# Decode attention backward on one Trainium2 core: two dV stores cut into a large part and two unequal rests

## The chip, the cores and the metric

The kernel runs on one core of a Trainium2 chip. The metric is the device time in microseconds (us) of one execution; lower is better. The core's engines run side by side: TensorE (PE, matrix products), VectorE (DVE), ScalarE (ACT), GpSimd (POOL) and SyncE (SP, which here only issues transfers), and 16 DMA engines that move data between the device memory (HBM) and the on-chip memory (SBUF, 128 partitions).

## The reference

One step of decode attention and its gradient: 32 heads, one query row each, 8192 keys and values of width 128, all bfloat16.

```python
def _fwd_reference(q, k, v):                  # q 1x32x1x128, k and v 1x32x8192x128
    scale = q.shape[-1] ** -0.5
    scores = jnp.einsum('bhqd,bhkd->bhqk', q, k) * scale
    attn = _softmax(scores, axis=-1)
    return jnp.einsum('bhqk,bhkd->bhqd', attn, v)

def reference(q, k, v, grad_out):
    ...
    _out, _vjp = jax.vjp(_f, q, k, v)
    _grads = _vjp(grad_out)
    return (out, dq, dk, dv)                  # in short
```

For a head with probabilities p (8192 of them) the outputs are out = p v, dV = p (outer) grad_out, dp = v grad_out, dS = p (dp - sum of p dp) times the scale, dQ = dS k and dK = dS (outer) q. K and V are read once (2 MB each for a head) and dK and dV of the same size are written, so every head moves 4 x 2 MB.

## The kernel before

**Layout.** A head's K lies in a tile `Kt` of 128 partitions x 64 slots x 128 numbers; partition p holds rows 64p to 64p + 63 of the head, which are 16 KB in one piece both in HBM and in the partition. `Vt` and the two gradient tiles `G_dk` and `G_dv` have the same layout. A load or store of a whole head is one transfer of 128 rows of 16 KB, issued by SyncE (`load_k`, L81; `load_v`, L85; the stores in `outer`, L266). K has three buffers, V two, each gradient two.

**Work of a head.** In the loop over h (0 to 32), step h does the first half of head h and the second half of head h - 1, in an order written out by hand (`tc.manual_schedule()`): VectorE transposes K in four blocks (`k_blocks`, `XK_sb`, L162), TensorE forms the scores (`k_scores`, L177), VectorE and ScalarE the softmax (`e`, `nbias`, `p_rep`), TensorE transposes V (`v_transposes`, L197) and forms dp (`v_scores`, L207), and `contract` (L231) accumulates out and dQ (`acc_p`, `acc_ds`). In between VectorE writes the outer products: `outer(h, which, r)` makes quarter r (16 slots) of dK or dV of head h in one VectorE instruction (L256) of 128 x 2048 numbers. After the last quarter it issues the store. For the first and the last head the store goes in two halves; for all others it is a single transfer after quarter 3:

```python
        if r % (4 // parts) == 4 // parts - 1:
            c = r // (4 // parts)
            nc.sync.dma_start(rows_of(dst, h, c, parts), slots(G, c, parts))
```

**Order on SyncE's queue.** In a step h: the store of dK of head h - 1 (after its quarter 3), the load of V of head h + 2 (`load_v`, in front of quarter 3 of dV), the store of dV of head h, then, in the next step, the load of K of head h + 3 (`load_k`), and so on. A load waits until its buffer is free, that is, until TensorE has done with the K or V that lay there. A first quarter of dV of head h writes a tile whose last store was that of head h - 2, and waits for that store. At the end `result` (L302) stores the two small outputs, 32 rows of 256 B each, from `fin_sb`; `out_0` in step 31 behind the stores of dV of head 31, `out_1` behind the stores of dK of head 31.

The functions that the change touches:

Of the kernel before, what the change touches and what calls it, by code (L numbers as in the profile page):

```python
# [19 lines left out]
K_BUFS = 3  # L20
V_BUFS = 2
QD = 32


@with_exitstack
def kernel(
# [11 lines left out]
    nc = tc.nc  # L38
    P = 128
    _, H, S, D = k.shape  # L40
    assert D == P and S % (P * CH) == 0 and H <= P
    NT = S // P
    NCH = NT // CH
    NQ = P // QD
    assert NCH == 4 and NQ == 4
    W = D // 2
    NB = W // QD
    scale = float(D) ** -0.5
# [20 lines left out]
    def rows_of(x, h, c, parts):  # L69
        L = NT // parts  # L70
        return x[0, h].rearrange("(p n) d -> p n d", p=P)[:, c * L:(c + 1) * L, :]

    def slots(X, c, parts):
        L = NT // parts
        return X[:, c * L:(c + 1) * L, :]
# [26 lines left out]
    nc.vector.memset(ones_f[:], 1.0)  # L102
    do_win = consts.tile([P, H, 2, QD + 2], BF16)
    nc.gpsimd.memset(do_win[:], 0.0)
    wins = {}
    for which in ("p", "ds"):
        wins[which] = []
        for i in range(2):
            w = consts.tile([P, NG, 2 * QD - 4], BF16, name=f"win_{which}{i}")
            nc.gpsimd.memset(w[:], 0.0)  # L110
            wins[which].append(w)
    q_win = []
    for i in range(2):
        w = consts.tile([P, 2 * NB, P + QD], BF16, name=f"win_q{i}")
        nc.gpsimd.memset(w[:], 0.0)
# [5 lines left out]
    q_blk = consts.tile([P, H, 2 * NB, NQ], BF16)  # L121
    four = consts.tile([H, 2 * NB, NQ, QD], BF16)
    for w in range(NB):
# [125 lines left out]
    def outer(h, which, r):  # L249
        x = st[h]  # L250
        if r == 0:
            x[which] = gpool.tile([P, NT, D], BF16, tag=which, name="G_" + which)
        G, dst = x[which], out_2 if which == "dk" else out_3
        rep, row = x["ds"] if which == "dk" else x["p"], qd[h][:, 0 if which == "dk" else 1, :]
        Q = NT // 4
        nc.vector.tensor_tensor(  # L256
            slots(G, r, 4).rearrange("p n (a b) -> p n a b", b=R),
            slots(rep, r, 4).unsqueeze(2).to_broadcast([P, Q, D // R, R]),
            row.rearrange("p (a b) -> p a b", b=R).unsqueeze(1).to_broadcast([P, Q, D // R, R]),
            op=ALU.mult)  # L260
        parts = 1
        if h == 0 or h == H - 1:
            parts = 2
# [3 lines that stand above are left out]
# [37 lines left out]
    for h in range(H + 1):  # L304
# [18 lines left out]
        if h > 0:  # L323
            ds_of(p_)
            outer(p_, "dk", 0)
            dq_of(p_, 0)
        if h < H:
            s_back(h)
        if h > 0:
            dq_of(p_, 1)  # L330
            outer(p_, "dk", 1)
            if p_ % ST == ST - 1:
                gather_copy("ds")
                gather(p_, "ds", st[p_]["m"])
# [9 lines left out]
        if h > 0:  # L344
            outer(p_, "dk", 2)
# [83 lines left out]
```

## Time and profile before

| What | us |
|---|---|
| median of 3 runs | 642.45 (642.36 to 643.0) |
| the profiled execution, whole | 642.33 |
| its span, first to last instruction | 640.5 |
| VectorE busy | 546.7 (85%) |
| TensorE busy | 466.5 (73%) |
| ScalarE busy | 205.5 (32%) |
| HBM read and written | 134.23 MB each, 419 GB/s over the span |

The profile's page gives busy times, the span in 40 slices, the DMA queues, the chain of waits that ended last, the costliest groups of instructions and the DMA issues. Other views answer questions on one stretch of time. In the slices each digit is the busy share of a slice in tenths; "DMA" is the mean busy share of the 16 DMA engines and "GB/s" what they moved. A view of one window divides that window into 40 slices. Times in views are from the span's start. The trace also records every packet of the DMA engines (start, length, size, queue, without the number of the engine) and every increment of a semaphore: each DMA engine that takes part in a transfer writes one such mark of 4 bytes when its share is done, and the transfer has landed when all its marks are there.

### The profile page before, as it was taken

To read this page: it belongs to the slowest core of one execution; us is meant where nothing else is said; L and a number is where in the kernel's file an instruction comes from. 1 tells how busy PE (TensorE), PEld (TensorE's weight loads), DVE (VectorE), ACT (ScalarE), POOL (GpSimd) and SP (SyncE) were. 2 spreads that over 40 slices of the span, in tenths; PEclk is the share of its full clock that TensorE was granted. 3 is DMA by queue.
4 is the path that set the end of the run, shared out by engine and by line. 5 is a ranking of instruction groups with operands and counts; after the bars stand their busy time and mean duration, and the time that the engine had idled before them with its cause. 6 is when DMAs were issued, how large, how long until landed. Compare 5 with 4: busy or idle time off the path is not lost.

```text
span 640.5 us, 8426 instructions
## 1 busy us (share of the span) xinstructions
PE 466.5 (73%) x3336; PEld 276.5 (43%) x3336; DVE 546.7 (85%) x780; ACT 205.5 (32%) x507; POOL 7.1 (1%) x13
## 2 busy tenths in 40 slices
PE   3776778778877867887866867767877687676771
PEld 1444444445544533455533444434554344444351
DVE  6799999998999999988889888898888988889871
ACT  1433332234433322334421333313442133322240
POOL 4000000000000000000000000000000000000000
PEclk9979888887787899877899887898787888879875
DMA  8999999999999999999999999999999999999994
GB/s 353 421 415 427 429 431 426 425 433 426 429 431 427 429 431 427 430 429 429 431 427 432 428 425 437 427 424 436 428 425 435 428 426 434 426 430 433 427 405 193
DMA packets 19671, 269.01 MB, mean 420 GB/s; under 512 B 2352, under 2 KB 2352, under 8 KB 2864
## 3 DMA queue, kind: packets, MB, share of 16 engines
q1 hardware_dynamic: 19536, 268.46, 98.6%
q8 instruction: 26, 0.43, 0.3%
q14 instruction: 13, 0.11, 0.0%
q10 hardware_dynamic: 96, 0.02, 0.0%
HBM read 134.23 MB, written 134.23 MB: 419 GB/s over the span
## 4 chain that ended last, share of the span: by engine, by line
DMA 45%; DVE 39%; PE 9%; ACT 4%; issue 1%; DVEq 0%; ACTq 0%
DMA Kt<-in_k_dram 45%; DVE XK_sb L162 15%; DVE G_dv L256 9%; DVE G_dk L256 7%; PE s_ps L177 3%; DVE dpT L214 2%; PE T_ps L197 2%; PE acc_ds L231 2%; ACT XV_sb L188 2%; DVE sT L184 1%; ACT p_rep L371 1%; DVE prod L217 1%; DVE ds L285 1%; ACT qd L273 1%; DVE four L125 1%
## 5 line engine op out<-in xcount | busy, mean ns | idle before, releaser
L197 PE MATMUL T_ps<-ident_f,Vt 128*128 128x128 f32 x1024 | 178.0, 339 | 1.0 <-DMA Vt<-in_v_dram 0.4
L256 DVE TENSOR_TENSOR G_dv<-p_rep,qd 128x2048 bf16<-128x2048 bf16 x128 | 148.2, 1220 | 35.3 <-DMA out_dram<-G_dv 28.1
L177 PE MATMUL s_ps<-XK_sb,win_q 128*128 128x512 bf16 x512 | 135.8, 397 | 50.1 <-DVE XK_sb L162 26.3
L197 PEld LDWEIGHTS T_ps<-ident_f,Vt 128*128 128x128 f32 x1024 | 151.4, 177 | 28.5 <-issue 20.1
L256 DVE TENSOR_TENSOR G_dk<-ds_rep,qd 128x2048 bf16<-128x2048 bf16 x128 | 154.7, 1210 | 1.1
L188 ACT COPY XV_sb<-T_ps 128x512 f32<-128x512 f32 x256 | 138.4, 586 | 53.2 <-PE T_ps L197 52.6
L162 DVE STREAM_TRANSPOSE XK_sb<-Kt 128x1024 f32<-128x1024 f32 x128 | 151.4, 1221 | 3.1 <-DMA Kt<-in_k_dram 2.9
L177 PEld LDWEIGHTS <-win_q 128*128 128x128 bf16 x512 | 52.7, 105 | 123.8 <-issue 83.2
L290 ACT COPY win_ds<-ds 128x64 bf16<-128x64 bf16 x32 | 7.8, 244 | 193.0 <-DVE ds L285 193.0
L355 ACT ACTIVATE e<-sT,nbias 128x64 f32<-128x64 f32 x32 | 13.0, 406 | 138.4 <-DVE nbias L350 138.4
L343 PE MATMUL m_ps<-ident_f,top 128*128 128x128 f32 x32 | 11.0, 342 | 60.3 <-DVE top L341 57.3
L207 PE MATMUL dp_ps<-XV_sb,do_win 128*32 128x512 bf16 x512 | 34.0, 382 | 24.7 <-ACT XV_sb L188 24.7
L231 PE MATMUL acc_p<-Vt,win_p 128*32 128x512 bf16 x512 | 48.3, 516 | 0.5 <-ACT win_p L372 0.5
L343 PEld LDWEIGHTS m_ps<-ident_f,top 128*128 128x128 f32 x32 | 4.5, 139 | 74.4 <-DVE top L341 72.9
L231 PE MATMUL acc_ds<-Kt,win_ds 128*32 128x512 bf16 x512 | 33.5, 382 | 0.9 <-ACT win_ds L290 0.9
L207 PEld LDWEIGHTS <-do_win 128*32 128x32 bf16 x512 | 14.2, 94 | 36.0 <-issue 29.5
L369 DVE RECIPROCAL rinv<-m_ps 128x1 f32<-128x1 f32 x32 | 5.4, 168 | 24.9 <-ACT qd L273 24.9
L184 DVE STREAM_TRANSPOSE sT<-s_ps 128x512 f32<-128x512 f32 x32 | 22.7, 709 | 3.6 <-PE s_ps L177 3.6
L356 PE MATMUL m_ps<-rs,ones_f 128*128 128x1 f32 x64 | 15.4, 310 | 11.5 <-ACT e L355 11.5
L231 PEld LDWEIGHTS <-win_p 128*32 128x32 bf16 x512 | 13.1, 117 | 23.8 <-issue 12.2
L214 DVE STREAM_TRANSPOSE dpT<-dp_ps 128x512 f32<-128x512 f32 x32 | 21.6, 675 | 0.8 <-PE dp_ps L207 0.8
L356 PEld LDWEIGHTS m_ps<-rs,ones_f 128*128 128x128 f32 x64 | 14.0, 272 | 17.8 <-ACT e L355 17.3
(57 smaller groups left out, 203.3 us busy)
## 6 DMA issues: line engine op xcount, KB each, us to landing
Vt<-in_v_dram SPq DMA_DIRECT2D x32, 2048.0 KB, 29.5
Kt<-in_k_dram SPq DMA_DIRECT2D x31, 2048.0 KB, 31.6
out_dram<-G_dv SPq DMA_DIRECT2D x30, 2048.0 KB, 34.8
out_dram<-G_dk SPq DMA_DIRECT2D x30, 2048.0 KB, 32.2
out_dram<-G_dv SPq DMA_DIRECT2D x4, 1024.0 KB, 11.6
out_dram<-G_dk SPq DMA_DIRECT2D x4, 1024.0 KB, 11.7
Kt<-in_k_dram SPq DMA_DIRECT2D x4, 512.0 KB, 5.6
out_dram<-fin_sb SPq DMA_DIRECT2D x2, 8.0 KB, 12.1
```

Of the source, the lines that this page charges most:

```text
L162: nc.vector.transpose(XK[h][:, :, :, u, :], slots(Kt[h], u, NCH).rearrange("p g d -> p (g d)").bitcast(F32).rearrange("p (g w j) -> p g w ...
L177: nc.tensor.matmul(st[h]["s"][:], lhsT=q_win[h % 2][:, c, at:at + P], rhs=cols[:, c // 2, u, c % 2], start=(u == 0 and c == 0), stop=(u == ...
L184: nc.vector.transpose(sT[:].rearrange("p g r -> p (g r)"), x["s"][:])
L188: nc.scalar.copy(XV[h][:, c * TB:(c + 1) * TB, :], st[h].pop(("T", c))[:])
L197: nc.tensor.transpose(T_ps[:, i, :], words[:, m * P:(m + 1) * P], ident_f[:])
L207: nc.tensor.matmul(out[b * QD:(b + 1) * QD, :], lhsT=do_win[:, h, e2, 2 - 2 * z:2 - 2 * z + QD], rhs=cols[:, z, e2, :, b * QD:(b + 1) * QD ...
L214: nc.vector.transpose(x["dpT"][:].rearrange("p m r -> p (m r)"), x["dp"][:])
L231: nc.tensor.matmul(acc[which][b * QD:(b + 1) * QD, :], lhsT=window(h, which)[:, g, at:at + QD], rhs=X[:, 4 * g:4 * g + 4, :].rearrange("p ...
L256: nc.vector.tensor_tensor(slots(G, r, 4).rearrange("p n (a b) -> p n a b", b=R), slots(rep, r, 4).unsqueeze(2).to_broadcast([P, Q, D // R, ...
L343: nc.tensor.transpose(x["m"][:, 128:256], top[:].to_broadcast([P, P]), ident_f[:])
L355: nc.scalar.activation(e[:].rearrange("p (u g) -> p u g", u=NCH), x["sn"], ACT.Exp, bias=nbias[:], scale=scale, accum_out=rs[:])
L356: nc.tensor.matmul(x["m"][:, 0:1], lhsT=ones_f[:], rhs=rs[:], start=True, stop=True, skip_group_check=True)
```

## The change

In `outer`, the dV stores of heads 20 and 24 leave in three transfers each instead of one. For head 20 the first has 48 of the 64 slots of all 128 partitions (rows of 12 KB); the other 16 slots (rows of 4 KB) go as partitions 0 to 123 and partitions 124 to 127. For head 24 the first has 56 slots (rows of 14 KB); the other 8 (rows of 2 KB) go as partitions 0 to 122 and 123 to 127. All three are issued after quarter 3, where the single store was. Everything else stays.

```diff
+SPLIT = {20: (16, 124), 24: (8, 123)}
...
             row.rearrange("p (a b) -> p a b", b=R).unsqueeze(1).to_broadcast([P, Q, D // R, R]),
             op=ALU.mult)
+        if which == "dv" and h in SPLIT:
+            if r == 3:
+                n, c = SPLIT[h]
+                to = dst[0, h].rearrange("(p n) d -> p n d", p=P)
+                nc.sync.dma_start(to[:, 0:NT - n, :], G[:, 0:NT - n, :])
+                for a, b in ((0, c), (c, P)):
+                    nc.sync.dma_start(to[a:b, NT - n:NT, :], G[a:b, NT - n:NT, :])
+            return
         parts = 1
         if h == 0 or h == H - 1:
             parts = 2
```

## The prediction

> **What bounds the kernel now.** The slices of the span come first.
>
> ```profile
> DVE  6799999998999999988889888898888988889871
> DMA  8999999999999999999999999999999999999994
> GB/s 353 421 415 427 429 431 426 425 433 426 429 431 427 429 431 427 430 429 429 431 427 432 428 425 437 427 424 436 428 425 435 428 426 434 426 430 433 427 405 193
> ...
> q1 hardware_dynamic: 19536, 268.46, 98.6%
> ```
>
> The 16 DMA engines are busy from the second slice to the last but one, at about 429 GB/s, and one queue (q1, SyncE's) carries it all. No engine that computes is near that. The chain of waits says the same in its last part: a K load of 32 us, a few us of work that lead to the next K load's issue, and so on.
>
> ```profile
> 567.39 31.98 DMA Kt<-in_k_dram
> 599.38 0.02 issue
> 599.40 3.50 DVE XK_sb L162 x3
> ```
>
> A load that takes 32 us where 2 MB need 4.9 us at 429 GB/s stands in a queue: about 27 us of older transfers are ahead of it. So a few us more or less in the issue of a transfer mean nothing; what counts is how much each of the 16 engines has to carry. They are not level. The DMA view of the last 16 us, in 40 slices of 0.4 us:
>
> ```profile
> DMA  6589998999999896422222111000000000000000
> GB/s 287 246 369 411 437 471 369 430 410 431 410 411 471 370 471 254 187 108 123 102 102 102 64 82 63 22 41 20 20 20 41 20 20 41 1 0 0 0 0 0
> ```
>
> One engine moves 429/16 = 26.8 GB/s. From 631.8 us some four engines are left (102 GB/s), after 635 us a single one (20 to 41), which works on to 638.9 us. SyncE waits for it:
>
> ```profile
> SPq L424 <- DMA out_dram<-fin_sb: 11.2, 1, 11.2
> ```
>
> The trace's landing records give every engine's place, since each engine writes one done-mark for each transfer (the page's 2,352 packets under 512 B are 139 x 16 marks and 128 rows of 256 B). The marks of the first small store, issued at 621.87, come after the first of them by 0, 0, 0, 0.1, 0.3, 2.0, then 3.9, 4.1, 4.2, 4.2, 4.3, 4.3, then 6.3, 7.1, 7.6, and 11.4 us. At the V load that lands at 23 us the same spread was an even ladder from 0 to 0.7 us. Two things made the lags. The page's code fetches (q8: 26 packets, q14: 13) each hold up the engine they fall on: a 16 KB fetch takes some 1.09 us and the packet behind it 1.08 instead of 0.61, so 1.6 us. And the last engine falls back steadily, from 5.0 us at 277 to 11.1 at 603: 1.9% slower than the rest in the long stretch (many of its 16 KB packets take 621 ns and more, for 611 elsewhere). Every load waits for its slowest engine, so this one also paces the chain.
>
> **The change, part by part.** It takes a quarter of head 20's dV store (0.5 MB) and an eighth of head 24's (0.25 MB) out of the two 2 MB stores, and sends them as stores of 124 + 4 and 123 + 5 rows. The bytes are the same, and the arithmetic is untouched.
>
> *What the remaining big stores save.* In every transfer of the trace the 16 engines take equal shares: 8 of 128 rows each. That stays so for the 48- and 56-slot parts. Packet times from the records: 611 ns for 16 KB, 309 for 8 KB, 159 for 4 KB, so 75.5 ns for each 2 KB between 8 and 16. Rows of 12 KB take 460 ns: 8 x 151 = 1.21 us less on each engine. Rows of 14 KB: 8 x 75.5 = 0.60 us less. Together 1.81 us for each engine that gets none of the small stores; 1.84 on the slow one.
>
> *Where the cut rows go.* No transfer of before has a row count that 16 doesn't divide. Bounds: dealt over all 16 engines (7 or 8 rows each), the change moves nearly nothing; all 124 rows on one engine would be 124 x 156 ns = 19.3 us. I take equal shares, since that is the only dealing the trace shows: 124 = 4 x 31 rows, 4 = 4 x 1, 123 = 3 x 41, 5 = 5 x 1. Packets follow each other 3 ns before the end of the last, so a 4 KB row costs 156 ns. Head 20 puts 31 x 156 + 156 = 4.99 us on four engines, with two marks 5.0, net of the saving +3.8. Head 24 puts 41 rows of 2 KB on three: about 81 ns each, on the line between 15 ns for 256 B and 159 for 4 KB (ends: 64 if only bytes counted at 159/4, 75.5 by the slope above, 156 if a row cost as much as 4 KB), so 3.3 + 0.1, net +2.8. Three engines get 6.6 us more (at 156 ns a row, 9.7), a fourth about +3.2, a fifth -0.5 for head 24, the rest -1.81.
>
> *Which engines.* The records carry no engine number. What they show: four of the five level engines at 598 us stand at 0, 0.06, 0.10, 0.15 us, which are the first rungs of the ladder at 23 us (0, 0.03, 0.07, 0.09, 0.12). So the engines served first in each transfer are those that no code fetch held up. If a transfer on few engines takes the first ones too, the load falls on engines with 11 us to spare. That is my choice.
>
> The Trainium skill, "DMA: Bandwidth & Descriptors", section "Why a DMA increments its semaphore by 16 and not by 1", says how the number of engines is chosen (the largest number up to 16 that divides both slowest dimensions) and that they are the lowest-numbered ones; no run here shows engine numbers. By it the dealing would be 4, 4, 3 and 5 engines. The same page speaks against such stores: "Rules for kernel authors" wants all 16 engines used through an outermost dimension that is a multiple of 16, and calls splitting a transfer by partitions pointless. If the extra 6.6 us stood on the path, that rule would make it 642.45 + 6.6 = 649.1, an estimate.
>
> *The sum.* Slow engine: 638.88 - 1.84 = 637.04. Loaded engines, if level: through with everything before the last two dK stores at 622.8 us, they now get there at 629.4, then carry 4.9 us (two 1 MB stores of 16 x 0.306 us in all), and end at 634.3, 2.7 us before the slow one. The next in line, 3.6 us ahead of the slow engine before, loses 1.81 as well. So the slow engine still ends last, 1.84 us earlier, and the loads at the end land as much earlier. Profiled execution: 642.33 (span 640.5 and 1.8 around it) - 1.84 = 640.5; the median of the runs shown is 0.12 higher, so 640.6.
>
> *Edits at nothing.* Two more issues on SyncE in each of two heads, 0.33 us each. Queued behind them is only the next K load, which waits for `acc_ds` anyway (issue of the store at 440.23, of the load at 448.00):
>
> ```profile
> SPq L81 <- PE acc_ds L231: 194.4, 28, 7.4
> ```
>
> Without that cover 4 x 0.33 = 1.3 us would come under 27 us of queue. The first product of dV of heads 22 and 26 now waits for three stores instead of one on VectorE, with the next head's K transposes queued behind it and TensorE's K scores behind those. It waits for the last mark, which is the slow engine's as long as the loaded ones lag less: 0.1 + 3.8 against 8.2 - 1.2 where head 20's store lands, 0.1 + 6.6 against 10.1 - 1.8 where head 24's does. So no wait gets longer.
>
> **The rivals.** *Slower: a loaded engine is one that already lags.* With +6.6 us an engine sets the end at its own lag + 6.6 against the 11.4 of before: below 3.0 us of lag nothing is lost, from 4.8 us on the kernel becomes slower. The three at 6.3, 7.1 and 7.6 would give +1.5 to +2.8 (644 to 645.3), the slow engine itself +6.6 (649). Drawn blind, three engines out of 16 would hit one of those four 6 times in 10 (1 - 220/560); the ladder speaks against a blind draw, and I give 16%. The skill's page, section "Latency and other measured facts", calls engines 7 and 15 the slow ones usually, which the trace can't confirm. *Part of the gain.* A loaded engine from the group at 3.9 to 4.3 ends at 10.5 to 10.9: 0.5 to 0.9 us gained, 641.6 to 641.9; 13%. (With 2 KB rows at their upper end a level engine comes to 9.7 against the slow one's 11.4 - 1.84 = 9.6, which costs only 0.1 of the gain.) *It does not do what it says.* If 124 rows are dealt over all 16, or the smaller packets cost more than the slope says, the balance stays: 642.4, 6%. The loaded engines could also fall behind only in the middle, at head 24; with 27 us of queue that delays a landing and not the end.
>
> **How the numbers follow.** Forecast 65%, with its own range 640.1 to 641.2 (1.2 to 2.3 us: a fetch that falls on another engine is 1.6 us, but only one on the slow engine matters). Measurement of this kernel can tell about 0.2%, or 1.3 us, from no change. The forecast passes that bound nearly always (0.62 of 0.65), the partial gain doesn't. So faster 0.62, same 0.22, slower 0.16. The range reaches from 639.9 into the lower half of the slower cases, 644.2.
>
> **What would show it.** In the profile after, the last packet should end near 637.0 instead of 638.9, again of a lone engine, and the pieces of the chain from head 24 on should come 1.8 us earlier. The marks of the last K load should still show the slow engine about 11 us behind the first, but three that stood level with the first should now stand some 8.4 us behind it (6.6 + 1.81). The 31 + 1 rows should show as 128 more packets of 4 KB and 128 of 2 KB. The cut stores should land no later than the K load before them. Wrong would be: an end set by an engine with many 4 KB packets, a last packet after 638.9 us, or marks of the 124-row store on all 16 engines.

## The result and the profile after

The changed kernel takes 641.47 us (median of 22 runs, 640.71 to 642.38); the kernel before, in 22 runs, 642.42 (641.96 to 643.0). The ratio is 0.9986, 95% interval 0.998 to 0.9992: about 0.95 us less, half of the 1.84 forecast, and inside the 0.2% that were taken as the bound of no change.

The page of the profile after, in the lines that answer to those of before:

```profile
span 639.3 us, 8433 instructions
...
DMA  8999999999999999999999999999999999999995
GB/s 351 420 428 428 427 427 430 426 431 426 427 428 429 430 427 432 427 433 427 430 427 432 430 426 432 430 424 422 430 432 426 429 429 428 430 431 430 427 413 218
DMA packets 19943, 269.01 MB, mean 421 GB/s; under 512 B 2368, under 2 KB 2368, under 8 KB 3136
...
q1 hardware_dynamic: 19808, 268.46, 98.8%
```

The transfers still bound the kernel. The count of packets under 512 B tells how the cut rows were dealt: 2368 are 16 more than the 2352 of before, and these 16 are done-marks: 4 + 4 + 3 + 5. The store of 124 rows went to four engines, that of 123 to three, as forecast. The DMA view of the last 16 us (slices of 0.4 us):

```profile
DMA  9998999999765444434321211210000000000000
GB/s 390 390 512 348 410 430 431 433 390 492 331 271 228 184 187 205 186 164 206 125 83 63 102 82 61 102 63 41 22 41 20 20 1 0 0 0 0 0 0 0
```

The last packet now ends at 637.87 us instead of 638.88, again of a lone engine. Before, the nine slices from 635.0 us on showed 20 to 41 GB/s, one engine; now several engines are at work until 636 or so, since the loaded ones come late too. In the landing records the marks of the last small store trail the first by up to 8.7 us, and the two engines ahead of the last by 7.0 and 6.4.

The chain of waits around the last K load is the old one, about 0.95 us earlier (the load landed at 599.38 before):

```profile
566.46 31.96 DMA Kt<-in_k_dram
598.43 0.02 issue
598.45 3.50 DVE XK_sb L163 x3
```

What the forecast did not have is on SyncE's queue. The first fence is its timeline behind head 20's dV store before (start, duration, line), the second the same place after the change, from the first small store on, and the third its waits after the change over the whole span (in total, times, longest):

```profile
400.62 0.33 SPq L266 DMA_DIRECT2D out_dram<-G_dv  x1
408.40 0.34 SPq L81 DMA_DIRECT2D Kt<-in_k_dram  x1
412.83 0.33 SPq L266 DMA_DIRECT2D out_dram<-G_dk  x1
418.30 0.34 SPq L85 DMA_DIRECT2D Vt<-in_v_dram  x1
```

```profile
400.73 7.43 SPq L268 DMA_DIRECT2D out_dram<-G_dv  x2
410.57 0.37 SPq L82 DMA_DIRECT2D Kt<-in_k_dram  x1
415.66 0.35 SPq L275 DMA_DIRECT2D out_dram<-G_dk  x1
420.57 0.34 SPq L86 DMA_DIRECT2D Vt<-in_v_dram  x1
425.47 0.33 SPq L275 DMA_DIRECT2D out_dram<-G_dv  x1
```

```profile
SPq L82 <- DMA Vt<-in_v_dram: 13.1, 4, 4.6
SPq L275 <- DMA out_dram<-G_dv: 12.5, 3, 4.7
SPq L433 <- DMA out_dram<-fin_sb: 6.7, 1, 6.7
```

Issues now come 4.9 us apart, the time of one 2 MB transfer: each waits until an older transfer has landed, which no issue of a store or a later load did before. The trace has eight landing semaphores for all of SyncE's transfers, used in turn, and never more than seven transfers are unlanded when an eighth is issued (before: mostly six). Small stores take places among these eight. Behind head 24's rests it was the issues themselves that took long: 6.4 us for the next K load (490.02 to 496.44), then 4.2, 4.0 and 3.2 us for the three transfers behind it. The queue is deep enough that the engines did not run dry here: K loads still land 29.8 us after their issue (median; 31.6 before), and in the DMA views from 428 to 444 and from 500 to 516 us no slice of 0.4 us is busy for less than six tenths.

**The slow engine's gain, read apart.** The share of time that a cut is worth can be read from one execution: the last mark of a K load, against the same mark before the change. Executions differ by up to a few us in their first half already, so what counts is the step between the K load in front of the first cut (head 22) and the last (head 31).

| Kernel | offset at K22 | offset at K31 | step | by its bytes |
|---|---|---|---|---|
| the change | -0.12 | -0.95 | -0.8 | -1.7 |
| e1_only20 | +0.32 | -0.70 | -1.0 | -1.2 |
| e2_only24 | +0.34 | -0.15 | -0.5 | -0.5 |
| e3_even112 | +2.45 | +2.61 | +0.2 | 0 |
| f1_eighths | -0.25 | -1.77 | -1.5 | -1.7 |
| f2_swapped | -0.12 | -1.46 | -1.3 | -1.7 |
| f3_five | +0.43 | +4.51 | +4.1 | +2.7 |
| g1_whole16 | -0.28 | -0.22 | +0.1 | 0 |
| g2_two8 | -0.12 | -0.93 | -0.8 | -1.1 |

(us; the slow engine's mark, which in f1 and f2 is not the last one at K31. "By its bytes" is worked out as in the prediction, with 0.1 us less relief where a rest of five rows is stored, since one of those rows turned out to be the slow engine's.) The change shows about half of what its bytes promise, the three eighths (f1) nearly all, the two (g2) most. Each line is one execution, and they do not all agree with the times: e1, the quarter alone, shows 1.0 of 1.2 here, while the median of its runs is only 0.5 us below that of the kernel before.

**Stretched packets.** The packet records show a second trace of the loss: packets at least 100 ns longer than usual for their size that do not follow a code fetch. From 400 to 470 us the kernel before has none; after the change there are 12, all from 430.6 to 441.6 us, while head 20's cut rows drain and in the transfers right behind them. They sum to 5.3 us over all engines; two of them, of 622 and 907 ns instead of 460, are by their place in time the slow engine's last 12 KB rows of that store.

### The profile page after: what moved, and what is told of

It reads as the page before. It is cut to its first block, busy times and chain, and to the rows that moved or that the text cites. A ratio compares the mean times of both kernels' runs of the same rounds, so it can differ in the third digit from the quotient of the medians.

```text
span 639.3 us, 8433 instructions
## 1 busy us (share of the span) xinstructions
PE 466.5 (73%) x3336; PEld 270.8 (42%) x3336; DVE 547.0 (86%) x780; ACT 204.7 (32%) x507; POOL 7.1 (1%) x13
## 2 busy tenths in 40 slices
DMA packets 19943, 269.01 MB, mean 421 GB/s; under 512 B 2368, under 2 KB 2368, under 8 KB 3136
## 4 chain that ended last, share of the span: by engine, by line
DMA 44%; DVE 35%; PE 13%; ACT 4%; issue 1%; DVEq 0%; ACTq 0%
DMA Kt<-in_k_dram 44%; DVE XK_sb L163 12%; DVE G_dv L257 8%; DVE G_dk L257 8%; PE s_ps L178 6%; PE T_ps L198 3%; DVE sT L185 2%; ACT XV_sb L189 2%; DVE dpT L215 2%; PE acc_ds L232 1%; PE acc_p L232 1%; ACT p_rep L380 1%; PE m_ps L365 1%; DVE ds L294 1%; DVE ds_rep L298 1%
## 5 line engine op out<-in xcount | busy, mean ns | idle before, releaser
L198 PE MATMUL T_ps<-ident_f,Vt 128*128 128x128 f32 x1024 | 171.4, 330 | 0.6
L178 PE MATMUL s_ps<-XK_sb,win_q 128*128 128x512 bf16 x512 | 139.3, 407 | 43.3 <-DVE XK_sb L163 22.3
L198 PEld LDWEIGHTS T_ps<-ident_f,Vt 128*128 128x128 f32 x1024 | 145.5, 171 | 28.4 <-issue 20.7
L365 PEld LDWEIGHTS m_ps<-rs,ones_f 128*128 128x128 f32 x64 | 12.7, 249 | 22.7 <-ACT e L364 22.7
## 6 DMA issues: line engine op xcount, KB each, us to landing
Kt<-in_k_dram SPq DMA_DIRECT2D x31, 2048.0 KB, 29.8
out_dram<-G_dv SPq DMA_DIRECT2D x28, 2048.0 KB, 31.6
```

Source lines behind the costliest of these rows:

```text
L178: nc.tensor.matmul(st[h]["s"][:], lhsT=q_win[h % 2][:, c, at:at + P], rhs=cols[:, c // 2, u, c % 2], start=(u == 0 and c == 0), stop=(u == ...
L198: nc.tensor.transpose(T_ps[:, i, :], words[:, m * P:(m + 1) * P], ident_f[:])
L365: nc.tensor.matmul(x["m"][:, 0:1], lhsT=ones_f[:], rhs=rs[:], start=True, stop=True, skip_group_check=True)
```

## The experiments

All edits are to the changed kernel, except g1, which edits the kernel before. Ratios are to the kernel before in the same batch of runs, with the 95% interval. In a `SPLIT` entry the first number is how many of the 64 slots are cut off, the second the number of partitions in the larger rest.

**One cut alone, and the same cuts dealt evenly.**

```diff
-SPLIT = {20: (16, 124), 24: (8, 123)}
+SPLIT = {20: (16, 124)}                    # e1_only20
+SPLIT = {24: (8, 123)}                     # e2_only24
+SPLIT = {20: (16, 112), 24: (8, 112)}      # e3_even112
```

> Only head 20's store is cut (48 slots whole, then 16 slots as 124 and 4 partitions). Theory A, the slow engine's share shrinks by 1.2 us but long packets near the cut store give 0.7 of it back: about 0.5 us less than before (641.9), with a cluster of stretched packets on several engines where the cut store drains. Theory B, the whole 1.2 us is gained and in the full change a loaded engine that comes close to the slow one eats the rest: 1.2 us less (641.2). Theory C, the gain came from transfers that are issued later: about half of the whole change's 0.95 us.

> Only head 24's store is cut (56 slots whole, 8 slots as 123 and 5 partitions). Theory A: 0.6 us less than before (641.8), the slow engine's relief of 8 x 75.5 ns, with no cluster of stretched packets. Theory B: also 0.6 us. Theory C: about half of 0.95 us.

> The same two stores cut at the same slots, but the rests as 112 and 16 partitions, which 16 engines can share equally: the same number of transfers and of bytes in small rows, and no engine relieved. Theories A and B: no gain, 642.4 within 0.3 us; the three cut transfers should each leave 16 marks. Theory C, the later issue is what helps: about 0.9 us less.

Measured: e1 641.93 us, ratio 0.9992 (0.9984 to 1.0001); e2 642.02, 0.9993 (0.9985 to 1.0002); e3 642.3, 0.9999 (0.999 to 1.0008). Neither half alone is clear of no change, and their 0.5 us each sum to the whole's 0.95. That is what theory A said. Theory B, the whole relief from each cut, is not supported for the quarter by the times (0.5 instead of 1.2), though e1's one profiled execution shows a step of 1.0. Theory C is hardly left: e3 has as many transfers, issues as late (against before, its K load of head 23 slips 2.3 us behind the one in front; in the change 2.4), and gains nothing. Its own stretched packets, counted below, are 0.3 us on a mean engine, so they could hide a part of such a gain, but not 0.9 us. The page of e3 shows that its dealing was even, 64 marks more than before, 16 for each added store:

```profile
DMA packets 19991, 269.01 MB, mean 418 GB/s; under 512 B 2416, under 2 KB 2416, under 8 KB 3184
```

The stretched packets: e1 has 9 of them from 431 to 443 us (2.8 us), e2 none there and two near its own cut (0.4 us in sum), e3 21 from 429 to 446 us (5.4 us). Each count is of one profiled execution. So the cluster comes with head 20's quarter, and uneven dealing is not needed for it.

**A map of the dealing.**

```diff
+SPLIT = {8 + i: (1, 127 - i) for i in range(15)}      # e4_map
```

> A look at the dealing. The dV stores of heads 8 to 22 are cut at the last slot (rows of 256 B), as 127 and 1 partitions for head 8, 126 and 2 for head 9, and so on to 113 and 15 for head 22. If a transfer's rows go in equal shares to the largest number of engines that divides the row count, counted from a fixed first engine, the smaller stores leave 1, 2, 3 ... 15 marks, each adding one engine, and the marks' times show where the slow engine stands: my forecast needs it outside the first four, and 12 of 15 sets without it if it is the thirteenth or later. If all rows are dealt over 16 engines, every transfer leaves 16 marks. Time: up to 1 us more than before, from the 30 more issues and some 10 us more for the first engine, which has 11 us to spare.

The smaller rests of 1, 2, ... 15 rows left 1, 2, ... 15 marks each, and the larger ones as many as the largest number up to 16 that divides them: 1 for 127, 14 for 126, 5 for 125, 15 for 120, 1 for 113. The four-row store was done at 258.15 us while the whole rows of the same head took their slowest engine until 259.50; the five-row store had its last mark at 279.30, behind the 279.10 of the whole rows. So the slow engine is the fifth in the dealing order. It gets nothing of a store on four engines or fewer, and a share of every larger one.

The time, 646.7 (one run), was 4.2 us worse, and not by the first engine's load. SyncE's timeline around the 127 rows on one engine, and the DMA view from 190 to 214 us (slices of 0.6 us):

```profile
173.40 20.67 SPq L268 DMA_DIRECT2D out_dram<-G_dv  x2
194.17 0.37 SPq L82 DMA_DIRECT2D Kt<-in_k_dram  x1
194.64 0.47 SPq L275 DMA_DIRECT2D out_dram<-G_dk  x1
195.20 0.38 SPq L86 DMA_DIRECT2D Vt<-in_v_dram  x1
```

```profile
DMA  9999998799799999989398999999999998999999
GB/s 434 432 431 431 403 430 335 314 370 332 272 381 382 410 410 382 410 191 328 137 382 355 437 437 437 437 451 437 410 437 437 437 437 382 410 409 432 431 431 431
```

The issue of the one-row store behind the 127 took 20.2 us, until 194 us; nothing behind it on SyncE could go out, and the other engines came to the end of their work: the rate falls to 137 GB/s, and the lags of the landing records shrink (from up to 3.8 us at 194 us to 2.3 at 202; at 217 eleven engines are within 0.6). So a transfer with many rows on one engine can hold up the issue of all that follow.

**Smaller cuts, exchanged cuts, the slow engine loaded.**

```diff
+SPLIT = {20: (8, 124), 22: (8, 124), 24: (8, 123)}      # f1_eighths
+SPLIT = {20: (8, 123), 24: (16, 124)}                   # f2_swapped
+SPLIT = {20: (16, 125)}                                 # f3_five
+SPLIT = {20: (8, 124), 22: (8, 124), 24: (8, 122)}      # f4_two
```

> The relief of the change, in three cuts of an eighth instead of a quarter and an eighth: heads 20 and 22 at 8 slots as 124 and 4 partitions, head 24 at 8 slots as 123 and 5. Every engine carries the same bytes as after the change. Theory D, it is the quarter cut (rows of 12 and 4 KB) whose surroundings take back part of the slow engine's relief: three times the 0.45 us of the eighth alone, so 1.4 us less than before, 641.1 or a little less, and few stretched packets. Theory E, each cut costs the slow engine about the same, by the later issues: not better than the change, 641.5 or more.

> The change with its two cuts exchanged: head 20 at 8 slots as 123 and 5 partitions, head 24 at 16 slots as 124 and 4. Theory D: the cluster of stretched packets moves from 430 us to about 510 us, with the quarter. Theory E: it stays behind the first cut, or comes at both. Time as the change, 641.5 within 0.5.

> Head 20 alone, a quarter cut as 125 and 3 partitions, which five engines share. By the marks of the change's five-row store and of the map, the slow engine is the fifth in the dealing order. It would then get 25 rows of 4 KB, 3.9 us, for the 1.2 it saves: 2.7 us more than before, 645.1. If the slow engine were one of the other eleven: 0.5 to 1.2 us less than before, 641.6.

> As the three eighths, but head 24's rest goes as 122 and 6 partitions, which two engines share: the third engine, which came within 1.6 us of the slow one after the change, gets 3 us less, and the first two 1.6 us more. If a loaded engine sets the end in a part of the change's runs, this is 0.3 us or more faster than the three eighths with 123; if the slow engine sets it, the two are alike within 0.2.

f1 takes 640.75 us, ratio 0.9975 (0.9966 to 0.9985), 1.67 us less than before: better than theory D's 1.4 and the best of the series (its interval still touches the change's). Its page counts 24 marks more than before, 4 + 4 + 4 + 4 + 3 + 5, and its last 16 us end at 637.2:

```profile
DMA packets 20079, 269.01 MB, mean 421 GB/s; under 512 B 2376, under 2 KB 2376, under 8 KB 3272
```

```profile
DMA  9999998997995554344231112112110000000000
GB/s 451 389 430 410 453 389 348 512 454 328 471 451 236 225 225 205 145 188 186 123 127 82 61 61 123 61 61 102 82 61 4 0 0 0 0 0 0 0 0 0
```

No lone engine is left: three work together to the end (61 to 102 GB/s in the last slices with work), and their marks of the last small store stand 7.0, 7.1 and 7.1 us behind the first. There is one stretched packet from 400 to 470 us and one later. And this in spite of stalls at SyncE no shorter than the change's: behind head 24's rests issues end up to 9.2 us later than before (8.4 in the change), and behind head 22's up to 6.8, where the change cuts nothing. Its timeline at head 24's rests:

```profile
481.14 14.84 SPq L268 DMA_DIRECT2D out_dram<-G_dv  x2
496.08 1.09 SPq L82 DMA_DIRECT2D Kt<-in_k_dram  x1
497.27 2.94 SPq L275 DMA_DIRECT2D out_dram<-G_dk  x1
500.30 4.17 SPq L86 DMA_DIRECT2D Vt<-in_v_dram  x1
505.08 3.72 SPq L275 DMA_DIRECT2D out_dram<-G_dv  x1
```

So late issues are not what cost the change its gain; theory E falls. Nor is it a loaded engine that ends last, since f1 puts the same bytes on every engine as the change does. f2 takes 641.36, ratio 0.9984 (0.9975 to 0.9994), as the change; its cluster has moved with the quarter: one stretched packet near head 20's eighth, 17 (5.6 us) from 511 to 527 us. That is theory D.

f3 takes 646.87, ratio 1.0073 (1.0059 to 1.0087): 4.45 us slower. The five engines that share 125 rows include the slow one (8 marks more than before, 5 + 3), and it sets the end alone. The DMA view from 625 to 645 us (slices of 0.5 us) shows it:

```profile
DMA  9899543379998998997211000000000000000000
GB/s 492 360 410 459 222 198 131 149 328 427 379 443 344 508 426 377 442 377 306 99 51 50 16 33 16 33 34 16 33 33 16 33 16 33 33 16 17 0 0 0
```

For 7 us nothing but that engine works. By bytes the loss was 2.7 us; the slow engine's mark fell back 4.2 us between the K loads of heads 22 and 23, in the stretch around the quarter cut where some 22 packets, from 428.8 to 447.3 us, were stretched.

f4 takes 641.52, ratio 0.9987 (0.9978 to 0.9996), slower than f1 and against both forms of its expectation. Sixty-one rows on each of two engines held up the issue of the six-row store for 17.5 us, until 504; the next K load then landed on its first engine 4.6 us later against before than the one in front, and some 40 packets from 508 to 515 us were stretched. It says nothing on the third engine.

**What in the quarter brings the cluster.**

```diff
+    nc.sync.dma_start(to[:, 0:NT - n, :], G[:, 0:NT - n, :])       # g1_whole16: head 20 alone,
+    nc.sync.dma_start(to[:, NT - n:NT, :], G[:, NT - n:NT, :])     # n = 16, no partition cut
...
+SPLIT = {20: (8, 124), 24: (8, 123)}                               # g2_two8
...
+    for m in (NT - n, NT - n // 2):                                # g3: head 20 alone, n = 16, c = 124
+        for a, b in ((0, c), (c, P)):
+            nc.sync.dma_start(to[a:b, m:m + n // 2, :], G[a:b, m:m + n // 2, :])
```

> Head 20's store cut only by slots: 48 slots and 16 slots, each of all 128 partitions, so no engine is relieved or loaded and one transfer more is issued. If rows of 12 and 4 KB alone bring the stretched packets, a cluster like that at 430 us comes here too; if the uneven dealing or the partition cut brings them, it does not. Time 642.4, or 0.3 more.

> The change with the quarter halved: heads 20 and 24 at 8 slots, as 124 and 4 and as 123 and 5. By its bytes the slow engine is relieved of 1.2 us instead of 1.8. Theory D (an eighth gives 0.45 to 0.6, a quarter hardly more): about 1.0 less than before, 641.4, as fast as the change itself, without the cluster. If the relief counted by its bytes alone: 0.6 slower than the change, 642.0.

> Head 20 alone: 48 slots whole (rows of 12 KB), and the last 16 slots as two eighths, each as 124 and 4 partitions (rows of 2 KB; five transfers). The same relief and load as the change's quarter. If the rows of 4 KB bring the cluster at 430 us, it is gone here; if those of 12 KB do, it stays.

g1 (one run, 642.07) has the rows of 12 and 4 KB and no stretched packet at all in that stretch. So it is not the row sizes alone; where issues did not stall for long (as in e4, f4 and g3), the cluster came only with a quarter cut by slots and by partitions, evenly dealt (e3) or not (e1). g2 takes 641.3, ratio 0.9982 (0.9973 to 0.9991): 1.2 us less than before, as fast as the change with a third less relief by bytes, and no stretched packet near head 20. Theory D held. g3 (one run, 641.88) was to tell rows of 4 KB from rows of 12 KB, and can't: four small stores in a row delayed the next K load's issue by 17 us, the mean rate from 420 to 436 us fell to 377 GB/s, and some 45 packets from 428.6 to 437.7 us were stretched, as in f4 after its long stall.

## Why the prediction was right and wrong

Right: the bound (16 engines with a queue, one of them behind), the dealing into equal shares on 4, 4, 3 and 5 engines, who sets the end (the slow engine in the profiled execution, and f3 shows that loading it moves the end), the direction, and that two more issues in a head cost nothing by themselves (e3). The range as a whole held the time, in part by luck: the forecast's own range, 640.1 to 641.2, did not, and the wide one held it because it also had to span the rivals. The nearest price was that of the rival "part of the gain" (641.6 to 641.9), but its reason, a loaded engine that ends last, is not what the profile after shows.

Wrong was the size, and with it the chance of 0.62 for more than 0.2%. The step that failed is the term of the sum that stands for the slow engine's saving, 1.84 us. In the profiled execution that engine gained 0.8. About 0.1 of the difference is the dealing: the fifth engine, for which the prediction has -0.5 at head 24, is the slow one itself. An eighth gave 0.4 to 0.5 of its 0.5 to 0.6 (e2; K24 in f1 and f2; g2 as a whole 0.8 of 1.1), three of them 1.5 of 1.7. The quarter gave about 0.5 of its 1.2 in the medians (e1 0.54; the change and f2 0.5 and 0.6 more than e2's 0.45), each with an interval of some 0.5 us to either side. Its row savings were taken for granted (460 ns for a 12 KB row, which is the usual length), while in the stretch around such a cut some packets on several engines take 0.1 to 0.9 us more; in the profiled execution 0.6 us of this fell on the slow engine's last two 12 KB rows. Which engines are hit differs between executions (the slow one lost little in e1, 1.4 us in f3). Why a quarter cut by partitions does this and an eighth doesn't is open. Uneven dealing (e3), late issues (f1) and the row sizes alone (g1) are not the whole cause. Not tested is whether it matters that a partition cut gives an engine other partitions than in a store of 128 rows (7 of 112 rows, for example, instead of 8 of 128).

The choice of the loaded engines was half right. The marks of the 124-row store come 0, 0.4, 2.6 and 4.3 us after the first of them; set against the marks of the transfers in front and behind, the four engines stood at 0, 0.4, 1.7 and 4.0 us when head 20's turn came. Only two were level. The ladder at the start told less than it was made to. The third engine, with 6.6 us more, ends 1.6 us ahead of the slow one after the change and level with it in f1, so the cut had little more to give than the 1.8 us asked.

Two readings of the trace were wrong in detail. The lines quoted for head 20 and head 24 (stores at 440.23 and 519.98) are those of heads 22 and 26; head 20's store was issued at 400.62 and landed with a lag of 7.5, head 24's at 479.92 with 9.4. Nothing in the sum hung on it. And "Edits at nothing" named the wait for `acc_ds` as cover and missed the limit of eight transfers in flight: issues slipped by 2 to 5 us behind head 20's rests and by up to 8.4 behind head 24's. The depth of the queue covered that, as the prediction had it; in e4, f4 and g3 it no longer did.

The Trainium skill's rule in "DMA: Bandwidth & Descriptors", section "Why a DMA increments its semaphore by 16 and not by 1" (the largest number of engines up to 16 that divides the rows), agrees with every count of marks here, from 1 for 127 rows to 15 for 120. What "Rules for kernel authors" advises against is two transfers of partition halves that both go over all 16 engines; rests dealt so gained nothing here (e3, 642.3), those dealt unevenly did (f1, 640.75). The note in "Latency and other measured facts", that engines 7 and 15 are usually slower than the others, can't be tested, since no run shows engine numbers; the slow engine is the fifth in the dealing order (e4, f3), which would be neither of the two if that order starts with the lowest-numbered engine, as the first section has it.

## What to carry to other kernels

When one queue feeds all DMA engines and never runs dry, as here, the kernel ends with the engine that gets through its share last, so look at the marks of a late transfer one by one: if one engine trails by several us, a few rows dealt to the others can shorten the kernel (by 1.67 us in f1, a quarter of a percent). What worked best in these runs were small pieces, at most some 30 to 40 rows on an engine and an eighth of a transfer at a time, with transfers of full width between them. A piece on too few engines, or several pieces at once, holds up the issue of everything behind it, and a store on one engine more than intended can load the very engine that should be relieved.

## What the runs showed of the hardware that was not expected

- The slow DMA engine is slow mostly in stores: between 280 and 600 us its lag grew by 0.16 us for each dV store, 0.13 for each dK store (0.10 without one jump of 0.62) and 0.03 to 0.04 for each load (kernel before, means over 16 or 17 transfers each).
- At most eight of SyncE's transfers are in flight here. In the changed kernel issues came 4.9 us apart where the extra stores had taken places.
- Rows piled on one engine block the issue itself: 2.8 us for the five-row store behind 41 rows on three engines (e2), 10.4 us for the third such cut (f1), 17.5 us behind 61 rows on two engines (f4), 20.2 us behind 127 on one (e4). With rests dealt over 16 engines (e3) no issue at heads 20 and 24 took more than 0.8 us.
- A quarter store cut by slots and by partitions stretched 9 to 22 packets by 0.1 to 0.9 us within some 19 us (the change, e1, e3, f2, f3); the same cut by an eighth did so to at most two, except in f4, where the issue had stalled. Each is one profiled execution.
